# A gated feed-forward block whose gate and up products are formed by Strassen's seven block products, in a ring of four single PSUM banks

## The chip, the cores and the metric

The kernel runs on one core of one Trainium2 chip. Its metric is the device time of one execution in microseconds (us). The core has a matrix engine (TensorE; PE in the profile, its weight loads PEld), three engines for elementwise work (VectorE or DVE, ScalarE or ACT, GpSimd or POOL) and SyncE (SP), which here only issues transfers. Each engine takes its instructions in the order in which the kernel gives them, and semaphores between the engines hold an instruction back until its inputs, and the buffer that it writes, are ready. TensorE writes only to PSUM, which has eight banks of 512 fp32 columns; POOL works in SBUF only.

## The reference

Two residual blocks follow each other on an input of 2048 tokens by 640 features, in fp32. The first one is spectral: a layer norm, a two-dimensional real FFT, a product with a complex filter, the inverse FFT. The second is a bilinear gated feed-forward block without a nonlinearity:

```python
def _B_ref(x, w_gate, w_up, w_down):
    g = jnp.einsum("bsd,df->bsf", x, w_gate)
    u = jnp.einsum("bsd,df->bsf", x, w_up)
    h = g * u
    return jnp.einsum("bsf,fd->bsd", h, w_down)

x = A_x
h = x + _A_ref(_layernorm(x, axis=-1), A_w_r, A_w_i)
h2 = h + _B_ref(_layernorm(h, axis=-1), B_w_gate, B_w_up, B_w_down)
```

The inner width is 1728, that is 13 column blocks of 128 and a last one of 64.

## The kernel before

All tokens stay in SBUF as 16 tiles X[0..15] of 128 tokens. The spectral part works through three stages: a transform over tokens (lines 250 to 283), a loop over 16 groups of columns (lines 388 to 420: `d_mm`, `s2_mm`, `filt`, `is2_mm`, `is2_out`), and the inverse over features, tile by tile (lines 578 to 594: `id_mm`, `unfold`, `is1_mm`, `acc`). The last stage also takes the layer norm of the second block for the tiles 0 to 7 along (`scale_shift`, `normalise`), and turns the tiles by TensorE so that features lie on partitions (`turn_mm`, then `turn_hi` on ACT and `turn_lo` on DVE).

Precision is kept by splitting. Each fp32 operand of the feed-forward block is held as a high part of fewer bits (fp32r) and a low part, value minus high. A product is three matmuls that accumulate in one PSUM bank: high by high, high by low, low by high. ACT makes the high part by a copy, POOL (for weights) or DVE (for activations) the low part by a subtraction.

The feed-forward block runs in two halves of 1024 tokens (`blk`), each of two quarters of 512 tokens (`sb`), which are the moving operand of a matmul. `xt` holds the turned tokens: [128 features, sb, 5 pieces of 128 features, high or low, 512 tokens]. The 14 column blocks c are taken in pairs, p = 0 to 6, c = 2p and 2p+1. For each c and each quarter `gu` (line 530) forms gate and up in the two banks of a pair of banks, 2 matrices x 5 pieces x 3 matmuls of 128x512; the block 13 holds gate and up in 64 columns each, 15 matmuls. Then `gate` (line 602) lets ACT copy up out of PSUM, DVE multiply, ACT write the product's high part into `hts` and DVE its low part. `down` (line 617) multiplies one tile of 128 tokens by the pair's two rows of blocks of the down weights, 12 matmuls of 128x320 (10 for the last pair), and DVE adds the result to X (`acc`, line 480). In the step of pair p the eight downs of the pair before it are issued between the two quarters of its first block, so that an even block has downs beside it and an odd block has none.

The order of the work is written out by hand: the lists `aside`, `dside` and `tside` say what ACT, DVE and the turning do in each round of the last spectral stage; `fill` is a queue of small layer norm operations of the tiles 8 to 15, of which one is issued after each down (`pop`); `late` is a gate's last subtraction, issued after other work. At the end of the first half (`close`, `turn`; lines 691 to 713) normalising, turning and downs of the tiles 8 to 15 are interleaved.

Weights come through `load_w` (line 428): SP loads a block of 128x1280 into one of two `stage` buffers, ACT writes the high part, POOL the low part, into one of two `wgu` (or `wd`) buffers. Block c+2 is loaded after block c. PSUM has two pairs of banks for gate and up (tag `eo`) and two for the downs (tag `y`). Working tiles of 640 columns come from a ring of six (`wk`).

Of the kernel before, what the change touches and what calls it, by code (L numbers as in the profile page):

```python
# [46 lines left out]
def tile_spectral_glu(ctx: ExitStack, tc: tile.TileContext, x, wf, wgu, wlast, wdown, wdlast,  # L47
# [6 lines left out]
    phase = ExitStack()  # L54
    stream = phase.enter_context(tc.tile_pool(name="stream", bufs=3))
# [4 lines left out]
    held = [None, None]  # L60

    def banks(name):
        if held[0]:
            held[0].close()
        held[0] = ExitStack()
        held[1] = held[0].enter_context(tc.tile_pool(name=name, bufs=2, space=bass.MemoryType.PSUM))

    def bank(tag, bufs=2):
        return held[1].tile([P, 512], F32, tag=tag, name=tag, bufs=bufs)

    def pair(tag, bufs=2):
        return held[1].tile([P, 2, 512], F32, tag=tag, name=tag, bufs=bufs)
# [20 lines left out]
    cit = keep.tile([P, P], F32, name="cit")  # L93
    ident = keep.tile([P, P], F32, name="ident")
    imt = keep.tile([P, 4, 161], F32, name="imt")
    irt = keep.tile([P, 5, NQ], F32R, tag="ic", name="irt")
    fmt = stream.tile([P, 675], F32, name="fmt", bufs=1)
    frt = stream.tile([P, 2, 2, NQ], F32R, name="frt", bufs=1)
    s1 = keep.tile([P, 4, NG, P], F32, tag="big", name="s1")
    s1r = keep.tile([P, 2, NG, P], F32R, tag="rem", name="s1r", bufs=2)  # L100
    fold = keep.tile([P, NR * 1026 + 2 * D], F32, tag="qm", name="fold")
# [95 lines left out]
    def scale_c(t):  # L197
        CR[t] = small.tile([P, P], F32, tag="cr", name="cr")
# [21 lines left out]
    banks("pone")  # L220
# [66 lines left out]
    def load_wm(g):  # L287
        m = stream.tile([P, 2, P], F32, name="mt")
        w = stream.tile([P, 2, 2, NQ], F32, name="wt")
        nc.sync.dma_start(m, mm[g, :, 0])  # L290
        nc.sync.dma_start(w, wf[g])
        WM[g] = (m, w)

    def load_wi(g):
        WI[g] = stream.tile([P, 2, P], F32, name="wi")
        nc.sync.dma_start(WI[g], mm[g, :, 1])

    qm = keep.tile([P, 4, NT, P], F32, tag="qm", name="qm")
    qr = keep.tile([P, 2, NT, P], F32R, tag="rem", name="qr", bufs=2)
# [8 lines left out]
    def d_mm(g):  # L308
        ps = PD[g] = bank("re"), bank("im")
        cut = ((1, 0), (0, 0), (1, 160), (0, 160))  # L310
        main = [(b, o, FW[c], s1[:, c, g], fmt[:, FOFF[c]:FOFF[c] + FW[c]]) for c, (b, o) in enumerate(cut)]
# [63 lines left out]
    def is2_out(g):  # L375
        pm, pr = PI[g]
        f = small.tile([1, P], F32, tag="f", name="f")
# [17 lines left out]
    for g in range(NG - 1):  # L395
        s2_mm(g)
        if g + 2 < NG:
            d_mm(g + 2)
        if g == NG - 2:
# [14 lines left out]
        if g == 6:  # L414
            nc.gpsimd.dma_start(irt, irem)
# [5 lines left out]
    phase.close()  # L421
    make_identity(nc, ident)

    wpool = ctx.enter_context(tc.tile_pool(name="wpool", bufs=2))
    xt = keep.tile([P, 2, 5, 2, 512], F32R, tag="big", name="xt")
    W = {}

    def load_w(key, src, n, engine=nc.gpsimd):
        st = wpool.tile([P, 1280], F32, tag="stage", name="stage")
        nc.sync.dma_start(st[:, :n], src)  # L430
        if key[0] == "d":
            w = keep.tile([P, 2, 1280], F32R, tag="rem", name="wd", bufs=2)
        else:
            w = wpool.tile([P, 2, 1280], F32R, tag="wgu", name="wgu")
        W[key] = w
        cuts = [(a, min(n, a + 640)) for a in range(0, n, 640)]
        his = [lambda a=a, b=b: act(w[:, 0, a:b], st[:, a:b], AF.Copy) for a, b in cuts]  # L437
        los = [lambda a=a, b=b: engine.tensor_tensor(w[:, 1, a:b], st[:, a:b], f32(w[:, 0, a:b]), op=OP.subtract)  # L438
               for a, b in cuts]
        return his, los  # L440

    def load_gu(c, engine=nc.gpsimd):
        if c < NC - 1:
            return load_w(("g", c), wgu[c], 1280, engine)
        else:
            return load_w(("g", c), wlast, 640, engine)

    def load_d(p):
        return load_w(("d", p), wdown[p] if p < 6 else wdlast, 1280)
# [54 lines left out]
    def turn_mm(t, tag="y"):  # L504
        ps = PT[t] = pair(tag)
        pv = ps.rearrange("p a b -> p (a b)")
        for k in range(5):
            nc.tensor.transpose(pv[:, k * P:(k + 1) * P], Z[t][:, k * P:(k + 1) * P], ident)  # L508

    def turned(t, l):  # L510
        sb, i = divmod(t % 8, 4)
        return (xt[:, sb, :, l, i * P:(i + 1) * P],
                PT[t].rearrange("p a b -> p (a b)")[:, 0:640].rearrange("p (k s) -> p k s", k=5))

    def turn_hi(t):
        hi, pk = turned(t, 0)
        act(hi, pk, AF.Copy)

    def turn_lo(t):
        lo, pk = turned(t, 1)  # L520
        tt(lo, pk, f32(turned(t, 0)[0]), op=OP.subtract)  # L521

    def transp(t, tag="y"):
        turn_mm(t, tag)
# [5 lines left out]
    def gu(c, sb, which=(1, 0), ks=range(5)):  # L530
        if 1 in which:
            ps = pair("eo")
            PG[c, sb] = ps[:, 0], ps[:, 1]
        w = W["g", c]
        if c < NC - 1:
            wv = w.rearrange("p l (k m f) -> p l k m f", k=5, m=2)
            sel = [(PG[c, sb][m], lambda l, k, m=m: wv[:, l, k, m]) for m in which]
        else:
            wv = w[:, :, 0:640].rearrange("p l (k f) -> p l k f", k=5)
# [7 lines left out]
    banks("pthree")  # L547
# [308 lines left out]
```

## Time and profile before

| | us |
|---|---|
| median of 3 runs | 764.21 |
| lowest and highest | 764.11, 769.02 |
| profiled execution, its own time | 764.33 |
| its span in the profile | 762.6 |

Busy times in the span: PE 742.3, PEld 645.1, DVE 321.5, ACT 264.5, POOL 171.0 us. The profile's page gives busy time by engine, the span in 40 slices, the transfer queues, the chain of work that ended last, and the costliest groups of instructions. A row of a group gives the source line, the engine, the operation, output and input by the program's names with their shapes, the count, then the busy time, the mean duration of one in ns, and the idle time of the engine ahead of them with what ended it. All matmuls of the feed-forward block are issued by one helper and so have line 81; their tiles tell them apart (`eo<-xt,wgu` gate and up, `y<-wd,hts` down). Rows of the timeline give the start in us, the time until the last of the merged instructions ended, the engine, the group and the count. A matmul's recorded duration overlaps the one behind it, so a matmul's price is read from start to start over many.

The feed-forward block begins on TensorE at about 178 us.

### The profile page before, as it was taken

To read this page: it belongs to the slowest core of one execution; us is meant where nothing else is said; L and a number is where in the kernel's file an instruction comes from. 1 tells how busy PE (TensorE), PEld (TensorE's weight loads), DVE (VectorE), ACT (ScalarE), POOL (GpSimd) and SP (SyncE) were. 2 spreads that over 40 slices of the span, in tenths; PEclk is the share of its full clock that TensorE was granted. 3 is DMA by queue.
4 is the path that set the end of the run, shared out by engine and by line. 5 is a ranking of instruction groups with operands and counts; after the bars stand their busy time and mean duration, and the time that the engine had idled before them with its cause. 6 is when DMAs were issued, how large, how long until landed. Compare 5 with 4: busy or idle time off the path is not lost.

```text
span 762.6 us, 9943 instructions
## 1 busy us (share of the span) xinstructions
PE 742.3 (97%) x4028; PEld 645.1 (85%) x4028; DVE 321.5 (42%) x595; ACT 264.5 (35%) x517; POOL 171.0 (22%) x156
## 2 busy tenths in 40 slices
PE   6899997999999999999999999999999999999998
PEld 5789886988898888989898988888898989898887
DVE  7956665896232322425241335332232414132334
ACT  4759997364412222031212335222203121212201
POOL 3301113331613122131113031312212121313000
PEclk9999999999999999999999999999999999999999
DMA  9305762100311111111101002411101111210003
GB/s 339 139 8 188 247 206 94 59 2 1 114 59 59 46 36 69 35 35 35 69 36 52 35 0 104 176 68 35 69 35 36 35 69 35 70 35 17 1 1 139
DMA packets 18622, 55.05 MB, mean 72 GB/s; under 512 B 2064, under 2 KB 6672, under 8 KB 18576
## 3 DMA queue, kind: packets, MB, share of 16 engines
q1 hardware_dynamic: 18000, 52.69, 19.8%
q0 software_dynamic: 288, 1.48, 0.5%
q8 instruction: 32, 0.52, 0.3%
q10 hardware_dynamic: 288, 0.23, 0.1%
q14 instruction: 14, 0.11, 0.0%
HBM read 49.16 MB, written 5.24 MB: 71 GB/s over the span
## 4 chain that ended last, share of the span: by engine, by line
PE 83%; ACT 7%; DVE 7%; issue 1%; DMA 1%; DVEq 0%; ACTq 0%
PE eo L81 51%; PE y L81 26%; ACT us L332 1%; ACT us L333 1%; DVE fold L178 1%; PE re L81 1%; PE im L81 1%; ACT qm L383 1%; DVE fold L183 1%; PE re L249 1%; PE u L325 1%; DVE x L485 1%; PE eo L508 1%; ACT qr L380 1%; ACT t L318 1%
## 5 line engine op out<-in xcount | busy, mean ns | idle before, releaser
L81 PE MATMUL eo<-xt,wgu 128*128 128x512 f32 x1620 | 381.6, 395 | 0.0
L81 PEld LDWEIGHTS eo<-xt,wgu 128*128 128x128 f32 x1620 | 302.8, 187 | 73.1 <-DVE xt L521 0.5
L81 PE MATMUL y<-wd,hts 128*128 128x320 f32 x1312 | 196.4, 309 | 0.2 <-DVE x L483 0.2
L81 PEld LDWEIGHTS y<-wd,hts 128*128 128x128 f32 x1312 | 193.5, 188 | 1.7 <-DVE x L483 0.4
L609 DVE TENSOR_TENSOR hb<-eo,u 128x512 f32<-128x512 f32 x52 | 35.9, 691 | 275.4 <-ACT u L608 275.4
L483 DVE TENSOR_TENSOR x<-y,x 128x640 f32<-128x640 f32 x119 | 97.9, 823 | 77.3 <-PE y L81 77.0
L438 POOL TENSOR_TENSOR wgu<-stage,wgu 128x640 fp32r<-128x640 f32 x52 | 81.4, 1585 | 218.9 <-ACT wgu L437 218.8
L608 ACT ACTIVATE u<-eo 128x512 f32<-128x512 f32 x52 | 31.0, 596 | 230.1 <-PE eo L81 230.1
L438 POOL TENSOR_TENSOR wd<-stage,wd 128x640 fp32r<-128x640 f32 x28 | 43.3, 1569 | 192.1 <-ACT wd L437 192.1
L437 ACT ACTIVATE wd<-stage 128x640 fp32r<-128x640 f32 x28 | 19.2, 732 | 130.7 <-PE y L81 118.0
L611 DVE TENSOR_TENSOR hts<-hb,hts 128x512 fp32r<-128x512 f32 x52 | 37.5, 721 | 27.2 <-ACT hts L610 27.2
L610 ACT ACTIVATE hts<-hb 128x512 fp32r<-128x512 f32 x52 | 32.9, 632 | 39.6 <-DVE hb L609 39.6
L437 ACT ACTIVATE wgu<-stage 128x640 fp32r<-128x640 f32 x54 | 36.7, 724 | 4.4 <-DMA stage<-in_wgu_dram 4.4
L194 PE MATMUL u<-cr,fold 128*128 128x128 f32 x192 | 29.5, 291 | 4.6 <-POOL fold L168 1.2
L194 PEld LDWEIGHTS u<-cr,fold 128*128 128x128 f32 x192 | 24.5, 193 | 8.9 <-DVE fold L183 4.2
L472 POOL TENSOR_TENSOR yt<-q 128x318 f32<-128x318 f32 x16 | 16.3, 1020 | 32.4 <-DVE q L469 21.4
L81 PE MATMUL eo<-imt,qm 128*128 128x161 f32 x128 | 20.4, 301 | 0.7 <-ACT qm L383 0.7
L385 POOL CAST qr<-f 1x128 fp32r<-1x128 f32 x16 | 4.5, 280 | 73.6 <-DVE qr L382 73.5
L336 DVE TENSOR_TENSOR y<-u,wt 128x322 f32<-128x322 f32 x30 | 14.8, 493 | 14.3 <-ACT us L333 9.2
L81 PEld LDWEIGHTS eo<-imt,qm 128*128 128x128 f32 x128 | 18.5, 190 | 2.6 <-issue 0.9
L325 PE MATMUL u<-t,mt 128*128 128x322 f32 x60 | 19.9, 453 | 0.6
L81 PE MATMUL y<-yt,cit 128*128 128x320 f32 x64 | 19.6, 432 | 0.0
(140 smaller groups left out, 593.6 us busy)
## 6 DMA issues: line engine op xcount, KB each, us to landing
stage<-in_wgu_dram SPq DMA_DIRECT2D x26, 640.0 KB, 3.9
wt<-in_wf_dram SPq DMA_DIRECT2D x16, 644.0 KB, 4.0
stage<-in_wdown_dram SPq DMA_DIRECT2D x12, 640.0 KB, 3.9
x<-in_x_dram SPq DMA_DIRECT2D x16, 320.5 KB, 6.5
out_dram<-x SPq DMA_DIRECT2D x15, 320.0 KB, 2.2
mt<-in_mm_dram SPq DMA_DIRECT2D x16, 128.0 KB, 3.8
wi<-in_mm_dram SPq DMA_DIRECT2D x16, 128.0 KB, 4.0
stage<-in_wdlast_dram SPq DMA_DIRECT2D x2, 640.0 KB, 3.8
```

The costliest lines, as they stand in the source:

```text
L81: nc.tensor.matmul(o, l, r, start=start, stop=stop, skip_group_check=True)
L194: nc.tensor.matmul(pm[:, k * P:(k + 1) * P], l, c, start=n == 0, stop=n == len(ls) - 1)
L325: nc.tensor.matmul(ps[h][:, 0:NQ], WM[g][0][:, h], T[g][:, h], start=True, stop=True)
L336: tt(y[:, h], ps[h][:, 0:NQ], w[:, 0, h], op=OP.mult)
L437: his = [lambda a=a, b=b: act(w[:, 0, a:b], st[:, a:b], AF.Copy) for a, b in cuts]
L438: los = [lambda a=a, b=b: engine.tensor_tensor(w[:, 1, a:b], st[:, a:b], f32(w[:, 0, a:b]), op=OP.subtract) for a, b in cuts]
L472: nc.gpsimd.tensor_tensor(view(y, 639, [[-320, 2], [-1, 159]]), q[:, 0::2, 1:160], q[:, 1::2, 1:160], op=OP.subtract)
L483: tt(xv, ps[:, :, 0:320], xv, op=OP.add)
L608: act(u, pu, AF.Copy)
L609: tt(hb, pg, u, op=OP.mult)
L610: act(hh, hb, AF.Copy)
L611: return lambda: tt(hl, hb, f32(hh), op=OP.subtract)
```

## The change

Twelve of the fourteen column blocks (0 to 11) are formed in another way in each half. The first four pieces of the 640 features are taken as two pairs, the two quarters of tokens as two columns, gate and up as two rows: a product of two 2x2 matrices of blocks, which Strassen's scheme in the form with shared sums does in seven block products instead of eight. The fifth piece of features is added to four of the products as before. Blocks 12 and 13 are formed directly as before, and come first in each half (`order = [6, 0, 1, 2, 3, 4, 5]`).

The operands of the seven products are prepared. For the tokens, `turn_hi` copies the first four pieces of the tiles 0 to 3 of a half also as fp32 (`TJ["b"]`), `turn_lo` of the tiles 4 to 7 adds two differences (`TJ[j]`), and `t_rest`, `t12` and `t34` form the remaining differences and split them, on DVE and ACT. The fifth piece of the later tiles is turned apart (`fifth`). For the weights, `prep(c)` works on one staging buffer: ACT and POOL split four pieces (1024 columns), POOL forms the combinations in place in the staging buffer by four operations, then ACT and POOL split 896 and 256 columns of these. The first part of `prep(c+1)` is issued after the second product of block c, the second part after its sixth; the load of block c+2 follows block c.

The products go in the order 1, 6, 7, 5, 3, 2, 4, each into one bank of a ring of four; the sums that turn them into gate and up, and the product of the two, are done by DVE in place in PSUM, with four working tiles (`p1`, `u2`, `u3`, `c22`) per block. `hts` has three slots of one block in place of two of two. The downs of the pair before are issued inside an even block: two after product 5, two after product 3, four after product 4; the last pair's downs follow at the end, the tile 7 last. At the start of the second half the tiles 8 to 15 are normalised in one piece inside block 11, and turned between the downs of the last pair.

Buffers are assigned by hand to named places (`home`), most of which are used again by later stages; the tables of the spectral part lie in such places, and the inverse table `irt` is loaded into the place of `xt`, after the last forward transform of the columns.

```diff
+    def single():
+        return bank("e", 4)
...
-            nc.gpsimd.dma_start(irt, irem)
...
+        if g + 3 == NG:
+            xt = home("big", [P, 2, 5, 2, 512], "xt", F32R)
+            irt = xt[:, 1].rearrange("p k l n -> p (k l n)")[:, 0:5 * NQ].rearrange("p (c q) -> p c q", c=5)
+            nc.gpsimd.dma_start(irt, irem)
...
     def turn_hi(t):
         hi, pk = turned(t, 0)
         act(hi, pk, AF.Copy)
+        if t % 8 == 0:
+            TJ["b"] = home("dA", [P, 4, 4, P], "bt")
+        if t % 8 < 4:
+            act(TJ["b"][:, t % 4], pk[:, 0:4], AF.Copy)
 
     def turn_lo(t):
         lo, pk = turned(t, 1)
         tt(lo, pk, f32(turned(t, 0)[0]), op=OP.subtract)
+        if t % 8 >= 4:
+            j = t % 4
+            d = TJ[j] = wk([P, 4, P], "tj")
+            b = TJ["b"][:, j]
+            tt(d[:, 0:2], pk[:, 0:2], b[:, 0:2], op=OP.subtract)
+            tt(d[:, 2:4], pk[:, 2:4], d[:, 0:2], op=OP.subtract)
...
+    def t_rest(j):
+        b = TJ["b"][:, j].rearrange("p (a k) n -> p a (k n)", a=2)
+        tt(b, b, view(TJ[j], 256, [[0, 2], [1, 256]]), op=OP.subtract)
...
+        def first():
+            wa, ws = W[c] = slot_of(c, blk)
+            act(wa[:, 0], stage[:, 0:1024], AF.Copy)
+            ptt(wa[:, 1], stage[:, 0:1024], f32(wa[:, 0]), op=OP.subtract)
+            ptt(stage[:, 640:896], stage[:, 640:896], stage[:, 1024:1280], op=OP.add)
+            ptt(stage[:, 896:1280], stage[:, 256:640], stage[:, 896:1280], op=OP.subtract)
+            ptt(stage[:, 384:640], stage[:, 640:896], stage[:, 384:640], op=OP.subtract)
+            ptt(stage[:, 0:256], stage[:, 0:256], stage[:, 384:640], op=OP.subtract)
+
+        def second():
+            wa, ws = W[c]
+            for a, b, o in ((384, 1280, 0), (0, 256, 896)):
+                act(ws[:, 0, o:o + b - a], stage[:, a:b], AF.Copy)
+            for a, b, o in ((384, 1280, 0), (0, 256, 896)):
+                ptt(ws[:, 1, o:o + b - a], stage[:, a:b], f32(ws[:, 0, o:o + b - a]), op=OP.subtract)
...
+        o1 = product(wa, 384, b11)
+        p1, u2 = wk([P, 512], "p1"), wk([P, 512], "u2")
+        act(p1, o1, AF.Copy)
+        o6 = product(ws, 0, t2)
+        at(0)
+        if ahead:
+            ahead[0]()
+        tt(u2, o6, p1, op=OP.add)
+        at(1)
+        o7 = product(ws, 640, [(t3[:, k, 0], t3[:, k, 1]) for k in range(2)])
+        u3, c22 = wk([P, 512], "u3"), wk([P, 512], "c22")
+        tt(u3, u2, o7, op=OP.subtract)
+        o5 = product(ws, 256, t1, [(wa, 896, b5[1])])
+        tt(u2, o5, u2, op=OP.add)
+        tt(c22, o5, u3, op=OP.add)
+        some(2)
+        at(2)
+        o3 = product(ws, 896, b22, [(ws, 512, b5[1])])
+        tt(o3, o3, u2, op=OP.add)
+        tt(o3, o3, c22, op=OP.mult)
+        act(hh[1], o3, AF.Copy)
+        at(3)
+        some(1)
+        tt(hl[1], o3, f32(hh[1]), op=OP.subtract)
+        some(1)
+        o2 = product(wa, 0, b21, [(wa, 256, b5[0])])
+        if ahead:
+            ahead[1]()
+        tt(p1, o2, p1, op=OP.add)
+        o4 = product(wa, 640, t4, [(wa, 896, b5[0])])
+        some(1)
+        tt(o4, o4, u3, op=OP.add)
+        tt(o4, o4, p1, op=OP.mult)
+        act(hh[0], o4, AF.Copy)
+        at(4)
+        some(2)
+        tt(hl[0], o4, f32(hh[0]), op=OP.subtract)
+        some(8)
+        at(5)
+
+    order = [6, 0, 1, 2, 3, 4, 5]
...
+            t1s = [t12(j) for j in range(4)]
+            late = gate_parts(NC - 2, 0, s12)
+            for j in range(4):
+                t1s[j][0]()
+                t_rest(j)
+            late()
+            gu(NC - 1, 1)
+            for j in range(4):
+                t1s[j][1]()
+            wdn = load_d(p)
+            late = gate_parts(NC - 1, 1, s13)
+            hi, lo = t34(0)
+            hi()
+            late()
+            lo()
+            if blk == 0:
+                second()
+            gu(NC - 2, 1)
+            gate_parts(NC - 2, 1, s12)()
+            for f in t34(1):
+                f()
+            issue(wdn)
...
+                side[2] = [lambda: low(range(8))]
```

In this diff `at(n)` issues what a block takes along at that place (the down weights' split at 3, the eight normalisations at 2, the next load at 5), `some(n)` up to n downs with what `fill` holds, `product` three matmuls for each pair of a weight piece and a token operand.

More of the change, by code (lines that the diff above doesn't have):

```diff
@@ L218, in s1_lo @@
            op=OP.subtract)
-    banks("pone")
+    banks("a", "pone")
     dve = [[] for _ in range(NT)]
@@ L643, in down @@
         acc(t, ps)
[L644 removed]
+        if last:
             nc.sync.dma_start(rows(out, t), X[t])
[L647 to L663 removed]
@@ L673, in tile_spectral_glu @@
         for ci in range(2):
             c = 2 * p + ci
-            first, turn, close = ci == 0 and n > 0, ci == 0 and n == 7, blk == 0 and c == NC - 1
-            if n or ci:
-                gu(c, 0)
-            late = gate(c, 0, slot, ci)
-            if first:
-                downs(prev, (4,) if turn else (0,))
-            late()
-            if n == 6 and ci == 0:
-                pop(len(fill))
-                for k in range(8, 12):
-                    lower(k)
-            if n == 0 and ci == 0:
-                issue(load_gu, 1)
-                issue(load_d, 0)
@@ L729, in tables @@
+            strassen(c, blk, slots[ci], ahead, downs if ci == 0 else [], side)
+            count += 1
+        prev = (blk, p, slots)
+    for j in (4, 5, 6, 0, 1, 2, 3, 7):
+        down(*prev, j, True)
+    open_pools["a"].close()
+    open_pools["y"].close()
 def tables():
```

368 lines of the change are left out of this document (213 added, 155 removed).

## The prediction

> **What bounds the kernel now.** First the page's busy times and slices, then the groups, then the engines by stretch, then the timeline of one step.
>
> ```profile
> span 762.6 us, 9943 instructions
> PE 742.3 (97%) x4028; PEld 645.1 (85%) x4028; DVE 321.5 (42%) x595; ACT 264.5 (35%) x517; POOL 171.0 (22%) x156
> PE 83%; ACT 7%; DVE 7%; issue 1%; DMA 1%; DVEq 0%; ACTq 0%
> ```
>
> TensorE is busy 97% of the span and holds 83% of the chain that ended last. Where, the stretches say:
>
> ```profile
> core 0: us, PE busy (x) PEld busy (x) DVE busy (x) ACT busy (x) POOL busy (x), PEclk, DMA share, GB/s
> 150.00:178.00 28.00, 27.39 (x162) 23.02 (x162) 26.70 (x71) 16.81 (x35) 8.99 (x9) 1.00 0.08 25
> 178.00:200.00 22.00, 22.00 (x104) 17.63 (x104) 8.84 (x14) 8.07 (x12) 7.13 (x5) 1.00 0.09 31
> 452.00:482.00 30.00, 29.81 (x179) 26.56 (x178) 17.17 (x23) 15.06 (x22) 6.19 (x4) 1.00 0.27 99
> 500.00:550.00 50.00, 50.00 (x251) 42.94 (x251) 13.42 (x18) 11.28 (x18) 12.39 (x8) 1.00 0.11 40
> ```
>
> The granted clock (column PEclk) is 1.00 throughout. From 178 us on TensorE never rests, with DVE, ACT and POOL near a quarter full. Before that, in the last spectral stage, DVE is as full as TensorE (26.70 of 28). The turn between the halves (452 to 482) costs 0.2. What one matmul costs there:
>
> ```profile
> L81 PE MATMUL eo<-xt,wgu 128*128 128x512 f32 x1620 | 381.6, 395 | 0.0
> L81 PEld LDWEIGHTS eo<-xt,wgu 128*128 128x128 f32 x1620 | 302.8, 187 | 73.1 <-DVE xt L521 0.5
> L81 PE MATMUL y<-wd,hts 128*128 128x320 f32 x1312 | 196.4, 309 | 0.2 <-DVE x L483 0.2
> 386.59 14.24 PE L81 MATMUL y<-wd,hts 128*128 128x320 f32 x96
> 400.67 28.16 PE L81 MATMUL eo<-xt,wgu 128*128 128x512 f32 x120
> 428.67 11.60 PE L81 MATMUL y<-wd,hts 128*128 128x320 f32 x78
> ```
>
> The mean of 395 ns overlaps its neighbour; from start to start 120 gate/up matmuls take 428.67 - 400.67 = 28.00 us, 0.2333 each, and 96 down matmuls 400.67 - 386.59 = 14.08, 0.1467 each. A step of two column blocks is 42.08 us.
>
> **The TensorE term.** A full column block needs 2 token halves x 2 matrices x 5 x 3 = 60 matmuls now. By Strassen it is seven products of 2 x 3 plus four pieces of 3 for the fifth part of D: 54. Twelve blocks in each half change, 12 and 13 do not: 24 x 6 = 144 fewer, 1620 to 1476. The 1312 down matmuls and the 80 transpositions stay. 144 x 0.2333 = **33.6 us less**. The Trainium skill ("TensorE: Matmul & The Clock Gate", "Back-to-back issue gap") gives about 131 ns as the sustained spacing of 512-column matmuls; by it the saving would be 18.9 us and the time 760.5. The trace does not agree: its 233 ns decides.
>
> **What takes its place, in the odd blocks.** A block with downs beside it lasts 7 products and 8 downs, 26.7 us. An odd one (c = 2p+1) has no downs: 54 x 0.2333 = 12.6 us, in which the next block's weights must be made. Its prices:
>
> ```profile
> L609 DVE TENSOR_TENSOR hb<-eo,u 128x512 f32<-128x512 f32 x52 | 35.9, 691 | 275.4 <-ACT u L608 275.4
> L608 ACT ACTIVATE u<-eo 128x512 f32<-128x512 f32 x52 | 31.0, 596 | 230.1 <-PE eo L81 230.1
> L610 ACT ACTIVATE hts<-hb 128x512 fp32r<-128x512 f32 x52 | 32.9, 632 | 39.6 <-DVE hb L609 39.6
> L437 ACT ACTIVATE wgu<-stage 128x640 fp32r<-128x640 f32 x54 | 36.7, 724 | 4.4 <-DMA stage<-in_wgu_dram 4.4
> L438 POOL TENSOR_TENSOR wd<-stage,wd 128x640 fp32r<-128x640 f32 x28 | 43.3, 1569 | 192.1 <-ACT wd L437 192.1
> L168 POOL TENSOR_TENSOR fold<-x 128x320 f32<-128x320 f32 x16 | 14.1, 891 | 19.8 <-DVE fold L183 8.4 <-DMA x<-in_x_dram 5.4 <-DVE ve L126 1.7
> stage<-in_wgu_dram SPq DMA_DIRECT2D x26, 640.0 KB, 3.9
> stage<-in_wlast_dram SPq DMA_DIRECT2D x2, 320.0 KB, 2.9
> L483 DVE TENSOR_TENSOR x<-y,x 128x640 f32<-128x640 f32 x119 | 97.9, 823 | 77.3 <-PE y L81 77.0
> 386.85 0.60 ACT L608 ACTIVATE u<-eo 128x512 f32<-128x512 f32 x1 [3.75 <-PE eo L81]
> ```
>
> POOL's two rows give 2.12 ns an element and 0.21 us a call: 1024 columns 2.38 us, 896 2.11, 384 1.03, 256 0.75. ACT's give 1 ns for each further element: 1024 1.11, 896 0.98. TensorE's result reaches the next engine 0.26 after the next matmul starts (386.85 to 386.59). From the block's start: products 1, 6, 7, 5, 3, 2, 4 end at 1.40, 2.80, 4.20, 6.30, 8.40, 10.50, 12.60. ACT copies product 1 (to 2.26), splits 1024 weights (to 3.37); POOL subtracts and forms four combinations, 2.38 + 3 x 0.75 + 1.03 = 5.66, to 9.1. DVE adds and multiplies on product 3 (8.66 to 10.08), ACT writes its high part (to 10.75) and, behind that in its queue, splits 896 combined weights (to 11.64); POOL subtracts them by 13.8, the last 256 by 14.6. The next block's second product wants those low weights at its third matmul, 12.60 + 1.40 + 0.47 = 14.47: **0.65 spare**. Product 4's bank is wanted again three products into the next block, 16.8; add, multiply, high part and low part release it at 15.7: 1.1 spare. The staging buffer refills from 14.6 and lands at 18.5, 5.9 into the long block; behind ACT's wait for it stands nothing before product 3's high part at 13.6. There POOL's 5.66 end at 11.7, the down weights' split (two of 1.57, behind ACT's part at 14.9) at 18.1, the combined weights at 21.1, and the next load lands at 25.0, before the odd block begins at 26.7. On SP the down weights (two loads of 2.9) stand behind the staging load: there by 8, wanted at 14. The adds are 11 DVE operations of 0.69 a block where there were four, 7.6 us; with eight accumulations of 0.82 a pair takes 21.8 of 39.3 us on DVE. So I take **0** for the steady state, and what gives way if the cover goes is TensorE, at once. DVE writing PSUM in place has no row. Excluding a time below a read's, it costs from 0.69 (the nearest row, taken) to twice that; then the chain is 1.4 longer, 0.7 late in each of 12 odd blocks, 9 us.
>
> **The spectral stage.** DVE sets its pace, so a third weight split and the differences for token block 4 count in full: 1.37 + 2 x 0.42.
>
> ```profile
> L438 DVE TENSOR_TENSOR wgu<-stage,wgu 128x640 fp32r<-128x640 f32 x2 | 2.7, 1372 | 0.0
> L382 DVE TENSOR_TENSOR qr<-ir,qr 64x256 fp32r<-64x256 f32 x14 | 5.9, 418 | 10.3 <-ACT f L381 10.3
> 117.16 0.31 PE L81 MATMUL im<-frt,s1r 128*128 128x322 f32 x1
> 131.72 0.58 PE L81 MATMUL eo<-irt,qr 128*128 128x322 f32 x2
> irt<-in_irem_dram POOLq DMA_DIRECT2D x1, 805.0 KB, 7.2
> ```
>
> Four ACT copies beside them lie within ACT's idle (16.81 busy of 28). **+2.0**, between 0 and 4.6 (with these copies at 0.6). The inverse table's load moves behind the last column transform (117.5), on POOL; it lands at 124.7, needed at 131.7: nothing. POOL's queue behind it holds one-row casts that nothing waits for before the last stage. SP's loads keep their ring of three, so the retagged buffers cost nothing.
>
> **The start of the first half.** Blocks 13 and 12 now run here with no downs, on four banks. I followed the queues, from 0 at the transposition of token block 4 (177.82 now).
>
> ```profile
> 177.82 0.77 PE y L508 x5
> 178.59 3.50 PE eo L81 x15
> 182.09 1.08 PE y L81 x4
> 201.29 3.10 POOL L438 TENSOR_TENSOR wd<-stage,wd 128x640 fp32r<-128x640 f32 x2 [1.81 <-ACT wd L437]
> 374.87 0.69 DVE L611 TENSOR_TENSOR hts<-hb,hts 128x512 fp32r<-128x512 f32 x1 [0.70 <-ACT hts L610]
> 204.49 3.43 POOL L438 TENSOR_TENSOR wgu<-stage,wgu 128x640 fp32r<-128x640 f32 x2
> 205.63 0.69 DVE L609 TENSOR_TENSOR hb<-eo,u 128x512 f32<-128x512 f32 x1 [0.69 <-ACT u L608]
> 207.02 1.45 DVE L611 TENSOR_TENSOR hts<-hb,hts 128x512 fp32r<-128x512 f32 x1 [0.70 <-ACT hts L610]
> 456.69 1.73 ACT L500 ACTIVATE zc<-x,b,r 128x640 f32<-128x640 f32 x2
> ```
>
> While POOL works, a DVE operation with both inputs in SBUF takes 1.45 instead of 0.69; one that reads PSUM does not slow down. (The Trainium skill, "SBUF — State Buffer", "Who interferes with whom", says that the former contends with POOL's reads and the latter does not; the trace agrees.) Strassen's adds read PSUM; the operand differences do not.
> - Block 12. TensorE: transposition 0.5, block 13 3.5, three inverse transforms 3.2, three transpositions of four 1.3, fifteen matmuls 3.5: at 12.0 it wants the bank that block 13's gate still reads. DVE: token block 5 (split 0.69, two differences 0.84) to 7.85, accumulation, gate product, accumulation to 10.2, a wait for ACT to 10.65, token blocks 6 and 7 (3.1), the gate's low part: 14.45. Wait **2.5**.
> - Its second token half. TensorE is at 14.5 + 3.5 + 0.4 (the fifth pieces) + 3.5 (block 13) + 3.5 = 25.4. ACT copies the fifth pieces, splits weights (20.2) and copies block 12 (20.8), DVE multiplies (21.5); then four differences at 1.45 beside POOL's weights (27.3) stand ahead of the low part that frees the bank: 28.0. Wait **2.6**.
> - Product 6 of block 0. TensorE wants its low weights at 28.0 + 3.5 + 1.4 + 0.47 = 33.4. DVE: four low parts, a product to 31.5; ACT: high part 32.1, operand split 33.2, combined weights 34.2; POOL 36.4. Wait **3.0**.
> - Product 7's bank, released 37.95 where TensorE is at 37.3: **0.65**. The down weights of blocks 12 and 13, split on POOL from 39.0 to 42.2, wanted at 41.45: **0.8**.
>
> Together **+9.5**; before, that stretch had no wait at all. It lies between 0 (the order of ready work may absorb them) and 19 (every late queue twice as late).
>
> **The turn.** Eight normalisations now stand in ACT's queue in one piece, 8 x 0.865 = 6.9 us (the row of two: 1.73), behind product 5 (from 6.56 after block 11's start to 13.5) and ahead of the high part of product 3, whose low part then ends on DVE at 14.9 and frees the bank. TensorE has done product 4 at 12.6 and the first transposition at 13.0, and wants that bank for the second: 1.9. The third down then wants a pair of banks whose accumulation stands on DVE behind the new tiles' splits (21.0 for 20.2): 0.8. Block 12's second half wants a bank that its first half's gate, behind four differences at 0.69, leaves 0.9 later. Sum 3.6 against 0.2 now, **+3.4**, between 0 and 7. The last down has 12 matmuls instead of 10, half of it behind the last bank: +0.15.
>
> **The sum** is made against the profiled execution's own 764.33 (span 762.6 and 1.73 around it; 0.12 above the median): 764.33 - 33.6 + 2.0 + 9.5 + 3.4 + 0.15 = **745.8 us**.
>
> **The rivals.** A, *all starts hidden*: 764.3 - 33.6 = 730.7. For it: 35 to 42% busy engines have room; against: the queues above are in order, and the banks fell to singles.
> B, *odd blocks a little late*: the chain misses by 0.7 to 1.2 us, 12 times, up to 14: 754 to 760. For it: 0.65 spare is thin; against: POOL's rows repeat to 0.02 us.
> C, *slower*: POOL's preparation becomes the bound. In odd blocks POOL's 5.66 and 2.11 us both stretch by a factor f; the later one ends at 3.45 + 7.77f. For 14.47 + 1.55 (12 x 1.55 = 18.5, the whole gain) f must be 1.62. At f = 2, 4.5 late, 12 times: 800. For it: DVE's 1.45; against: POOL's pair went only from 3.10 to 3.43 there, f = 1.1.
> D, *the matmuls saved are worth less*: if the weight loads set the pace, a matmul saved is worth its load, 0.187: 26.9 instead of 33.6, 752.5. For it: the loads are busy 85% of the span; against: spacing goes with the moving columns (0.2333 at 512, 0.1467 at 320) at equal loads.
>
> **Chances.** Forecast 0.55, A 0.17, B 0.16, C 0.07, D 0.05. Faster by over 1% (about what a measurement of this kernel tells from no change) means under 756.6: the forecast but for an upper tail 0.51, A 0.17, a part of B 0.06, D less its tail 0.04: 0.78. Slower: C's upper part, 0.05. The rest, 0.17. The range leaves out A's end and C, and takes in D and B up to 759: 734 to 759; the likeliest case alone is 738 to 752.
>
> **What would show it.** Right: 1476 matmuls of 128x512 at 0.233; 39.3 us per pair of blocks; TensorE waits of 2 to 3 us by DVE and POOL at the start of the first half, near 2 at the turn. Wrong: a TensorE wait repeating every 39 us (B; above 1.5 us each, C), none anywhere (A), a saving per matmul under 0.2 us (D).

## The result, and the profile after

The changed kernel takes 735.0 us (median of 4 runs, 734.25 to 737.35) where the kernel before takes 766.4 on the same chip (764.11 to 769.02). The ratio is 0.959, 95% interval 0.955 to 0.964. Forecast were 745.8 us, 734 to 759. The profiled execution took 734.25 us, 732.5 of them span.

Some executions, of the kernel before too, are 1 to 5 us longer, with one more fall of the clock in the spectral part; two of the four behind the 766.4 are of this kind, and the account below sets 764.33 against 734.25, both without it.

The page of the changed kernel:

```profile
span 732.5 us, 10144 instructions
PE 704.9 (96%) x3884; PEld 620.4 (85%) x3884; DVE 454.4 (62%) x803; ACT 277.9 (38%) x540; POOL 299.5 (41%) x275
...
PEclk9999999999989999999999999999999999999999
```

TensorE is still busy 96% of the span. DVE rose from 321.5 to 454.4 us and POOL from 171.0 to 299.5, and neither became the bound. New is the digit 8 among the clocks, in the twelfth of the 40 slices (201 to 220 us). The groups of TensorE with 512 columns, with the count ahead of the bar:

```profile
L82 PE MATMUL e<-xt,wst 128*128 128x512 f32 x864 | 206.8, 390 | 0.0
...
L82 PE MATMUL e<-t,wst 128*128 128x512 f32 x288 | 74.9, 395 | 4.3 <-ACT wst L693 2.7 <-POOL wst L695 1.6
L82 PE MATMUL e<-xt,wdir 128*128 128x512 f32 x180 | 41.9, 391 | 1.1 <-DVE q L475 1.1
L82 PE MATMUL e<-ht,wst 128*128 128x512 f32 x144 | 37.8, 399 | 0.0
```

864 + 288 + 180 + 144 = 1476 matmuls of 512 columns, as counted ahead. What one costs is read from start to start. This is the timeline of one pair of blocks in the steady state; the second column reaches to the end of the last matmul and is not the price:

```profile
315.62 1.55 PE L82 MATMUL e<-xt,wst 128*128 128x512 f32 x6
317.01 1.52 PE L82 MATMUL e<-t,wst 128*128 128x512 f32 x6
318.37 1.52 PE L82 MATMUL e<-ht,wst 128*128 128x512 f32 x6
...
325.47 0.60 ACT L790 ACTIVATE ht<-e 128x512 fp32r<-128x512 f32 x1 [6.72 <-DVE e L789]
...
326.99 2.82 POOL L695 TENSOR_TENSOR wst<-raw,wst 128x896 fp32r<-128x896 f32 x2 [2.19 <-ACT wst L693]
...
329.25 1.52 PE L82 MATMUL e<-t,wst 128*128 128x512 f32 x6
...
334.01 3.68 PE L82 MATMUL y<-wd,ht 128*128 128x320 f32 x24
337.52 2.23 PE L82 MATMUL e<-xt,wst 128*128 128x512 f32 x9
...
354.24 1.55 PE L82 MATMUL e<-xt,wst 128*128 128x512 f32 x6
```

Six matmuls take 318.37 - 317.01 = 1.36 us: **0.2267 each, where the kernel before needed 0.2333**. A down matmul stayed at (337.52 - 334.01) / 24 = 0.146. The pair takes 354.24 - 315.62 = 38.62; 108 x 0.2267 + 96 x 0.1467 are 38.56. So nothing waits there. The forecast of 39.3 was right about the waits and wrong about the price.

The longest waits of TensorE from 178 to 240 us (in total, times, longest), and the busy times of a stretch behind them:

```profile
PE e L82 <- ACT wst L693: 2.7, 1, 2.7
PE e L82 <- POOL wst L695: 1.6, 1, 1.6
PE e L82 <- DVE q L475: 1.1, 1, 1.1
```

```profile
core 0: us, PE busy (x) PEld busy (x) DVE busy (x) ACT busy (x) POOL busy (x), PEclk, DMA share, GB/s
212.65:225.00 12.35, 12.35 (x51) 10.52 (x52) 6.93 (x11) 3.48 (x5) 9.80 (x8) 0.77 0.31 108
```

TensorE stands still for 2.70 and 1.63 us, and then it is slow: from 212.65 to 225 it is busy throughout and its granted clock is 0.77 on average (more exactly, one half up to 218.21 and full behind it). The start of the first half shows both:

```profile
188.47 7.18 PE L82 MATMUL e<-xt,wdir 128*128 128x512 f32 x30
...
193.25 0.68 DVE L639 TENSOR_TENSOR ht<-e,ht 64x512 fp32r<-64x512 f32 x1
...
195.74 10.48 PE L82 MATMUL e<-xt,wdir 128*128 128x512 f32 x45
...
198.59 5.62 DVE L556 TENSOR_TENSOR bt<-bt,tj 128x512 f32<-128x512 f32 x4
...
206.06 1.52 PE L82 MATMUL e<-xt,wst 128*128 128x512 f32 x6
210.28 0.73 PE L82 MATMUL e<-t,wst 128*128 128x512 f32 x2 [2.70 <-ACT wst L693]
212.65 2.07 PE L82 MATMUL e<-t,wst 128*128 128x512 f32 x4 [1.63 <-POOL wst L695]
214.52 2.76 PE L82 MATMUL e<-ht,wst 128*128 128x512 f32 x6
219.68 3.09 PE L82 MATMUL y<-wd,ht 128*128 128x320 f32 x20
```

The 19 matmuls from 212.65 to 219.68 take 7.03 us; at 0.2267 they are 4.31. The fall of the clock costs 2.7 us there. In the turn between the halves two waits are left:

```profile
445.02 0.66 PE L518 MATMUL e<-ident,zt 128*128 128x128 f32 x4 [0.67 <-DVE ht L793]
451.00 2.03 PE L82 MATMUL y<-wd,ht 128*128 128x320 f32 x12 [0.49 <-DVE x L489]
```

**The account.** Against a run in which every stretch takes its matmuls' price, the changed kernel loses 0.8 us ahead of the first transposition of token block 4 (178.64, was 177.82), 1.6 to 206.06, 8.2 from there to 238.27 (32.21 us where the matmuls' price is 23.97), 1.9 in the turn, 1.1 in the steady stretches and 0.9 at the end: 14.5. The kernel before lost 1.1 in the same way, 0.4 of it in the turn and 0.6 at the end. So 764.33 - 33.6 (144 matmuls fewer) - 9.8 (the other 1476 cheaper by 0.00667 each) + 13.4 = 734.3, and 734.25 were measured. The forecast had no 9.8, and 15.05 in place of 13.4.

### The profile page after: what moved, and what is told of

It is laid out like the page before. It is cut to its first block, busy times and chain, and to the rows that moved or that the text cites. A ratio compares the mean times of both kernels' runs of the same rounds, so it can differ in the third digit from the quotient of the medians.

```text
span 732.5 us, 10144 instructions
## 1 busy us (share of the span) xinstructions
PE 704.9 (96%) x3884; PEld 620.4 (85%) x3884; DVE 454.4 (62%) x803; ACT 277.9 (38%) x540; POOL 299.5 (41%) x275
## 4 chain that ended last, share of the span: by engine, by line
PE 77%; DVE 11%; ACT 10%; issue 1%; DMA 1%; POOL 0%; DVEq 0%; ACTq 0%
PE e L82 44%; PE y L82 26%; PE eo L82 2%; ACT us L343 2%; ACT us L344 2%; DVE fold L190 1%; ACT qm L394 1%; PE re L261 1%; DVE x L489 1%; DVE fold L195 1%; DVE bt L556 1%; PE im L82 1%; PE re L82 1%; ACT t L331 1%; ACT t L330 1%
## 5 line engine op out<-in xcount | busy, mean ns | idle before, releaser
L82 PE MATMUL e<-xt,wst 128*128 128x512 f32 x864 | 206.8, 390 | 0.0
L82 PE MATMUL y<-wd,ht 128*128 128x320 f32 x1312 | 201.4, 310 | 1.2 <-DVE x L489 1.1
L82 PEld LDWEIGHTS y<-wd,ht 128*128 128x128 f32 x1312 | 195.3, 188 | 5.7 <-DVE x L489 2.7
L82 PEld LDWEIGHTS e<-xt,wst 128*128 128x128 f32 x864 | 160.7, 188 | 31.7
L684 POOL TENSOR_TENSOR wst<-raw,wst 128x1024 fp32r<-128x1024 f32 x24 | 57.8, 2409 | 169.6 <-ACT wst L683 169.6
L695 POOL TENSOR_TENSOR wst<-raw,wst 128x896 fp32r<-128x896 f32 (+1 forms) x48 | 67.9, 1438 | 27.8 <-ACT wst L693 27.8
L82 PE MATMUL e<-t,wst 128*128 128x512 f32 x288 | 74.9, 395 | 4.3 <-ACT wst L693 2.7
L82 PEld LDWEIGHTS e<-t,wst 128*128 128x128 f32 x288 | 55.0, 191 | 16.7 <-ACT wst L693 3.1
L445 POOL TENSOR_TENSOR wd<-draw,wd 128x640 fp32r<-128x640 f32 x28 | 44.4, 1608 | 47.7 <-ACT wd L444 47.7
L82 PE MATMUL e<-xt,wdir 128*128 128x512 f32 x180 | 41.9, 391 | 1.1 <-DVE q L475 1.1
```

What stands on the lines that cost most here:

```text
L82: nc.tensor.matmul(o, l, r, start=start, stop=stop, skip_group_check=True)
L445: los.append(lambda r=r, a=a, b=b: engine.tensor_tensor(w[:, 1, a:b], r, f32(w[:, 0, a:b]), op=OP.subtract))
L684: ptt(wa[:, 1], stage[:, 0:1024], f32(wa[:, 0]), op=OP.subtract)
L695: ptt(ws[:, 1, o:o + b - a], stage[:, a:b], f32(ws[:, 0, o:o + b - a]), op=OP.subtract)
```

## The experiments

Two things were to be explained: why a matmul became cheaper, and what the start of the first half really loses.

**Why 0.2267.** The same matmul, with the same operand shapes, became 7 ns shorter. The change gives the weight buffers other sizes and thereby other places in SBUF. In the kernel before the moving operand starts 32 bytes past a multiple of 64 and the weights on one; in the changed kernel both start 32 past. (Distance means below: the start of the weights less that of the moving operand, as it lies past a multiple of 256 bytes. It is 224 in the kernel before and 0 in the changed one.) My first theory was that equal places past a multiple of 64 bytes make the difference. The rival was that something in the order of the products does. The first run moves the buffers of the kernel before and changes nothing else:

```diff
+    padding = ctx.enter_context(tc.tile_pool(name="padding", bufs=1))
+    nc.gpsimd.memset(padding.tile([P, 8], F32, name="pad"), 0.0)
...
```

> The kernel before, with one unused strip of 32 bytes ahead of the gate and up weights, so that their high and low parts start 32 bytes past a 64-byte line, as the moving tokens already do. Nothing else moves on TensorE. Theory, place in SBUF: the spacing of the 128x512 matmuls falls from 0.2333 to the 0.2267 of the changed kernel, 1620 x 0.0067 = 10.8 us less, about 753.5. Rival, the single PSUM banks or the new layout of the weights made the matmuls faster: spacing stays 0.2333 and the time about 764.

Measured: 755.58 us against 764.64, ratio 0.987 (0.983 to 0.990).

```profile
398.14 27.39 PE L81 MATMUL eo<-xt,wgu 128*128 128x512 f32 x120
425.36 4.85 PE L81 MATMUL y<-wd,hts 128*128 128x320 f32 x32
```

120 matmuls now take 425.36 - 398.14 = 27.22 us, 0.2268 each, where they took 28.00. 32 bytes of padding are worth 9 us to the kernel before. The reverse, the changed kernel with its weights 32 bytes further on in their buffers:

```diff
-        w = home("wB" if (c + blk) % 2 == 0 else "wA", [P, 4352], "wst", F32R)
-        return cut(w, 0, 2, 1024), cut(w, 2048, 2, 1152)
+        w = home("wB" if (c + blk) % 2 == 0 else "wA", [P, 4368], "wst", F32R)
+        return cut(w, 8, 2, 1024), cut(w, 2056, 2, 1152)
```

(`wdir` likewise: [P, 3856], its parts at 8 and 1288. The larger buffers also move what lies behind them, so that the distances in this run are 32, 96, 160 and 224.)

> The changed kernel with only the gate and up weights moved by 32 bytes within their buffers, onto a 64-byte line, while the tokens stay 32 bytes past one: the offsets of the kernel before. Place in SBUF: spacing 0.2333 in all 1476 matmuls, 9.8 us more, about 744. Rival, single banks: spacing 0.2267, 734.

Measured: 743.06 us (742.53 to 743.67), 8.1 more than the changed kernel. Six matmuls take 320.86 - 319.46 = 1.40 again:

```profile
319.46 1.56 PE L82 MATMUL e<-t,wst 128*128 128x512 f32 x6
320.86 1.56 PE L82 MATMUL e<-ht,wst 128*128 128x512 f32 x6
```

The third run puts both operands on multiples of 64 bytes and leaves the distance at 0 (32 bytes of padding ahead of both, and a table ahead of both widened by 64):

```diff
+    nc.gpsimd.memset(keep.tile([P, 8], F32, name="pad"), 0.0)
...
-    tab = home("stage", [P, 1448], "tab")
+    tab = home("stage", [P, 1464], "tab")
```

> The changed kernel with a strip of 32 bytes ahead of all reused buffers, so that tokens, weights, products and down weights all start on a 64-byte line. If only an equal offset of the two operands matters: spacing 0.2267 and 0.1467 as now, 734. If the moving operand also pays for its own offset: 512 columns below 0.220 and 320 columns below 0.140, 12 to 25 us less, 710 to 722. If neither matters: 734.

Measured: 734.76 us, the spacing still 1.36 for six. So a start on a multiple of 64 bytes is worth nothing; the place of the one relative to the other counts. The modulus of 64 was only a guess so far, and a later run was made to test it, with another shift in every odd block:

```diff
-        return cut(w, 0, 2, 1024), cut(w, 2048, 2, 1152)
+        o = (0, 1, 0, 2, 0, 4, 0, 8, 0, 16, 0, 32)[c]
+        return cut(w, o, 2, 1024), cut(w, 2048 + o, 2, 1152)
```

> The changed kernel with the weights of the odd column blocks alone shifted inside their buffer, by another distance in each: block 1 by 4 bytes, 3 by 8, 5 by 16, 7 by 32, 9 by 64, 11 by 128 (the staged matrix's even blocks stay). Where weights and moving columns start at the same distance past a multiple of 64 bytes, six matmuls take 1.36 us, where they differed by 32 they took 1.39 to 1.40. Theory, only equality past a multiple of 64 bytes counts: blocks 1, 3, 5 and 7 at 1.40 a product, 9 and 11 and all even blocks at 1.36; eight slow blocks of 54 matmuls give 432 x 0.006 = 2.6 us, 737.6. Rival, the price comes in steps of 32 bytes: block 7 alone slow (and 0.7 us in all, 735.7). Rival, it depends on the distance between the operands as a whole: 9 and 11 slow too.

Measured: 739.67 us (one run), 4.7 more than the changed kernel, and not as expected. In the first half, blocks 9 and 11, shifted by 64 and 128 bytes, were slow as well, and so were even blocks with no shift: the buffers had grown by 128 bytes, and this had moved one of the two by 128 against the tokens. An even block shows it by itself. Its products 6 and 7 use the same weights buffer, with moving operands from two buffers; the distance is 128 for product 6 and 0 for product 7:

```profile
291.46 1.56 PE L82 MATMUL e<-t,wst 128*128 128x512 f32 x6
292.86 1.54 PE L82 MATMUL e<-ht,wst 128*128 128x512 f32 x6
294.23 1.55 PE L82 MATMUL e<-t,wst 128*128 128x512 f32 x6
```

Product 6 takes 292.86 - 291.46 = 1.40 and product 7 294.23 - 292.86 = 1.37. So the rule must have 256 in it, not 64, and that was put to a test in which the two rules forecast different things: the padding of the first run at 96 and at 288 bytes (the second line with 72 in place of 24):

```diff
-    nc.gpsimd.memset(padding.tile([P, 8], F32, name="pad"), 0.0)
+    nc.gpsimd.memset(padding.tile([P, 24], F32, name="pad"), 0.0)
```

> The kernel before with its weight buffers 96 bytes further on (the first run moved them by 32). From the weights' start to that of the moving columns it is then 64 bytes past a multiple of 256, and 0 past a multiple of 64. Theory after the run by blocks, the spacing is 0.2267 us only where the two starts are equal past a multiple of 256 bytes: no gain, 0.2333 and 764 to 765 us. The older theory, equal past a multiple of 64 bytes is enough: 0.2267 and 755.6.

> The same with 288 bytes: the two starts are then equal past a multiple of 256 bytes (and of 512). Both theories: 0.2267 us and 755.6, as the first run (32 bytes, equal past a multiple of 256 as well). A third, that only the very place of the first run is good: 764 to 765.

Measured: 765.15 us with 96 bytes (ratio 0.999, 0.997 to 1.001) and 754.79 with 288 (0.987, 0.983 to 0.991). The first two rows are of 96 bytes, the others of 288:

```profile
401.87 28.17 PE L81 MATMUL eo<-xt,wgu 128*128 128x512 f32 x120
429.87 10.42 PE L81 MATMUL y<-wd,hts 128*128 128x320 f32 x70
```

```profile
396.71 27.39 PE L81 MATMUL eo<-xt,wgu 128*128 128x512 f32 x120
423.94 14.24 PE L81 MATMUL y<-wd,hts 128*128 128x320 f32 x96
```

28.00 and 27.23 us for 120. The older theory fell. Where weights and moving operand start equally far past a multiple of 256 bytes, 512 columns settle at 0.2267 us in every run. At most other distances tried they take 0.231 to 0.2333 (whole kernels at 64 and 224; blocks at 4, 8, 16, 32, 96, 128, 136, 144 and 160), and some 0.229 at 192. But the run by blocks also has an exception, which the two theories leave out. In its second half, block 1 has its weights at a distance of 132. The first row holds thirty of its matmuls and six of the next block, at 0:

```profile
517.93 8.32 PE L82 MATMUL e<-xt,wst 128*128 128x512 f32 x36
526.09 1.52 PE L82 MATMUL e<-t,wst 128*128 128x512 f32 x6
```

526.09 - 517.93 = 8.16 us for 36 is the low price, 0.2267, while the six matmuls ahead of them, also at 132, took 0.233 each. So an equal place is enough for the low price and is not shown to be needed. Why the chip does so no run shows.

**What the start of the first half loses.** TensorE waits 4.3 us for the combined weights of block 0, and the clock falls. The theory: DVE's and POOL's queues are late, and the clock falls because TensorE stands still. The first attempt issues those weights ahead of block 13's second gate:

```diff
             late()
+            if blk == 0:
+                second()
             gu(NC - 1, 1)
...
             lo()
-            if blk == 0:
-                second()
```

> The changed kernel with the second part of block 0's weight preparation issued ahead of block 13's second token half in the first half, not behind the operand split. Theory: product 6 of block 0 waits for these weights (2.70 for ACT, 1.63 for POOL) and the granted clock falls behind that wait; both go, 4.3 + 2.7 = 7 us less, about 727, clock 1.00 throughout. Rival: the clock falls for what runs there, not for the wait: 4.3 less, 730, with a stretch at about 0.8 left. Second rival: the split moved up holds back block 13's gate on ACT and the wait only moves there: 733.

Measured: 733.86 us, against 735.0 within the spread. The weights are early now, and TensorE waits almost as long for something else:

```profile
205.56 4.94 DVE L560 TENSOR_TENSOR t<-tj,t 128x512 fp32r<-128x512 f32 x4
...
212.49 2.93 PE L82 MATMUL e<-t,wst 128*128 128x512 f32 x6 [4.09 <-DVE ht L639]
```

The four low parts of L560 now run beside POOL's subtractions and take 4.94 us where they took 2.48, and the low part of L639 stands behind them and holds the bank. The clock fell here too (0.87 from 212.65 to 225), for half as long. The wait had moved, so the thing to remove was the late work on DVE. The four differences of L556 (5.62 us at 198.59) need nothing that isn't there at 193.9; they only stood behind the split of the fifth pieces, which waits for TensorE:

```diff
     late()
+    for j in range(4):
+        t_rest(j)
     gu(NC - 2, 0)
     fifth((5, 6, 7))
...
                 t1s[j][0]()
-                t_rest(j)
+                if blk == 1:
+                    t_rest(j)
```

> The four DVE differences of L556 of the first half (1.4 us each beside POOL, 198.59 to 204.2) move ahead of the fifth pieces, into DVE's idle stretch from 193.9 to 196.6. Theory, DVE's and POOL's queues make the wait: the four take 0.7 each, everything behind them on DVE ends some 2.9 us earlier, the combined weights' high part ends near 208.1 instead of 210.3 and the low part near 210.4 instead of 212.6; TensorE wants them at 207.4 and 208.5, so 0.7 + 1.9 = 2.6 of wait is left where there were 4.3, and the time is 735.0 less 1.7 to 3, about 732.5. Rival, another wait takes its place as in the run before: 734 to 735.

Measured: median 731.13 us; 729.49 and 729.57 in two executions, 732.69 and 733.08 in the others, the profiled one among them, whose clock was 0.64 between 125 and 135 us. Its times below lie some 4 us later for that reason.

```profile
198.25 2.50 DVE L556 TENSOR_TENSOR bt<-bt,tj 128x512 f32<-128x512 f32 x4
...
214.06 1.20 PE L82 MATMUL e<-t,wst 128*128 128x512 f32 x4 [1.63 <-POOL wst L697]
215.09 1.53 PE L82 MATMUL e<-ht,wst 128*128 128x512 f32 x6
```

The four take 2.50 us in place of 5.62. The wait for ACT's high part is gone, that for POOL's low part is the old 1.63, and the four matmuls behind it take 215.09 - 214.06 = 1.03 us where they took 1.87: the clock holds (1.00 from 206 on). From the first product of block 0 to that of block 1 this trace takes 237.09 - 210.33 = 26.76 us in place of 32.21: 5.5 less, 2.7 for the wait and about as much for the clock. The two short executions are 4.7 below the 734.25; where the other 0.7 went isn't shown. Both edits together:

> The same, and the combined weights of block 0 earlier as in the run before. Theory that two late things stood one behind the other, and that the clock fell because TensorE paused: low weights are there by 207.7 and block 13's second gate frees its bank near 206.5, so under 0.5 us of wait is left of 4.33; the granted clock stays at 0.99 or over from 205 to 225 us, where it was 0.90 and 0.77; 4 + 2.7 gained, 728.3. Rival, the clock falls there for another reason (the hour of the run, the load of the other engines): 0.77 again, 731. Rival, the wait moves a third time: 733 to 735.

Measured: median 729.79, three of the four within 729.34 to 730.14. No wait for the weights is left, but four small ones of 0.57, 0.44, 0.29 and 0.38 (the bank of block 13's second gate, that of block 12's, and the down weights) add up to 1.68, as much as the run before had. Its stretch in the place of the slow one:

```profile
212.65:225.00 12.35, 11.68 (x65) 10.21 (x64) 9.45 (x17) 4.59 (x8) 10.98 (x9) 1.00 0.01 2
```

The clock is 1.00. So the fall belongs to the pauses, and the thirteen traces together say more about it. In each of them the clock changes on a raster of 3.413 us, whose start differs from execution to execution: it is one half for one, two or three such steps, and full otherwise. The rows show single steps: the length, the time for which TensorE was busy, and the granted clock. The first two are of the changed kernel, the third of the run with the differences first, the last of the kernel before with 288 bytes of padding:

```profile
207.97:211.38 3.41, 0.73 (x2) 1.00 0.00 0
211.38:214.79 3.41, 2.15 (x5) 0.50 0.13 20
124.48:127.90 3.42, 1.52 (x15) 1.00 0.52 196
124.85:128.26 3.41, 1.54 (x12) 1.00 0.00 0
```

In the changed kernel TensorE stands still for 3.41 - 0.73 = 2.68 us of the step, and the clock is one half in the next. It also falls behind the third row, with 1.89 us, but not behind the fourth, with 1.87. Taken over all steps at full clock in the thirteen traces, up to the last matmul, a fall follows each of the twelve in which TensorE stands still for 1.89 us or more, and none of the others. So it is the idle time in sum within one step that goes with a fall, and not the length of one pause. This fits the spectral part too: all versions have a pause of 1.89 us there, which lies within one step in six traces, where the clock falls, and is cut by the end of a step in the other seven, where it doesn't. No run was made to test this, and other loads may have another limit.

**How thin the steady state is.** The forecast found 0.65 us spare on the combined weights in odd blocks. The trace has 0.63: the third matmul of product 6 starts at 329.25 + 2 x 0.2267 = 329.70, and POOL's 896 columns, which take 2.08 from 326.99 (2.82 less 0.74 for the last 256), end at 329.07. One more subtraction on POOL should show it:

```diff
+            if c > 0 and c % 2 == 0:
+                ptt(ws[:, 1, 0:640], stage[:, 384:1024], f32(ws[:, 0, 0:640]), op=OP.subtract)
             for a, b, o in ((384, 1280, 0), (0, 256, 896)):
                 ptt(ws[:, 1, o:o + b - a], ...)
```

> A subtraction of 640 columns (1.57 us) is repeated on POOL ahead of the low part of the combined weights, in the blocks without downs only: 10 in the run (the successors of c = 1, 3, 5, 7, 9 in each half). Theory, 0.63 us is spare there: TensorE waits 0.9 to 1.0 for POOL 10 times, 735.0 + 9.4 = 744.4, and a pair of blocks takes 39.5 us instead of 38.6. Rival, POOL has room that the trace does not show: 735. Rival, each wait also lowers the clock as the long one at 210 us did, by a few us each: above 755.

Measured: 746.31 us (745.79 to 746.55), 11.3 more. The wait list and one odd block:

```profile
PE e L82 <- POOL wst L697: 10.9, 11, 1.6
```

```profile
330.99 0.61 PE L82 MATMUL e<-t,wst 128*128 128x512 f32 x2
...
332.53 1.20 PE L82 MATMUL e<-t,wst 128*128 128x512 f32 x4 [0.93 <-POOL wst L697]
333.56 1.53 PE L82 MATMUL e<-ht,wst 128*128 128x512 f32 x6
```

10.9 less the 1.6 of the start are ten waits of 0.93, where 0.94 were worked out. Each costs more than its length: the product takes 333.56 - 330.99 = 2.57 instead of 1.36, 1.21 more. After a pause four matmuls take 1.03 in place of 0.91. Ten times 1.21 is 12.1, somewhat above the 11.3 measured. The clock did not fall behind these ten.

**The other waits.** The two edits that removed the wait for the weights, and two for waits elsewhere: block 13's first matmuls behind the inverse transform of their tile (the wait of 1.12 for L475), and the normalisations of the turn in two groups of four:

```diff
-            gu(NC - 1, 0)
         is1_mm(t)
+        if t == NT - 3:
+            gu(NC - 1, 0)
...
-                side[2] = [lambda: low(range(8))]
+                side[2], side[3] = [lambda: low(range(4))], [lambda: low(range(4, 8))]
```

> The last but one, with two more edits: block 13's first 15 matmuls stand behind token block 13's inverse transform instead of ahead of it (a TensorE wait of 1.12 for DVE at the reopened banks), and of the eight normalisations in block 11 four stand behind product 5 and four behind the high part of product 3 (waits of 0.67 and 0.49 at the turn). Theory, each wait has its own cause and none takes its place: 728.3 less 1.1 less 0.7 to 1.2, about 726.3. Rival, DVE paces the last spectral tiles anyway and ACT the turn: the two give nothing, 728.3.

Measured: 727.94 us (median of 6, 727.3 to 731.73), ratio to the kernel before 0.950 (0.947 to 0.953). That is 1.9 under the run with the first two edits, as expected. That run had come out 1.5 above its own expectation of 728.3, and so this one is 1.6 above the 726.3. The waits of 1.12 for L475 and of 0.67 for L793 are gone from the list. It is the fastest version of the study.

## Why the prediction was right, and where it was not

The forecast was 745.8 us, the time 735.0: inside the range, near its lower end, outside the likeliest case's own 738 to 752.

- **The matmuls saved: 33.6 us.** The count was right (1476). The step that failed is the price: "0.2333 each" was carried from the kernel before to the changed one, as if it belonged to the shape. It belongs to the shape and to the place of the operands. All 1476 became 0.0067 us cheaper, 9.8 us, by an accident of the buffers' sizes. Compared at equal places (the kernel before with 32 or 288 bytes of padding, 755.2 on average), the change gains 20.2 us: 144 x 0.2267 = 32.6 less 12.4 of costs. Rival D, a saved matmul worth its weight load of 0.187, is not what is seen: the spacing is 0.2267 with loads of 188 to 194 ns.
- **The steady state: 0.** Right, and with the right margins: 0.65 forecast and 0.63 found; 0.8 us were lost over some 415 us, without a wait on the list. Product 3's high part began 325.47 - 315.62 = 9.85 after the block's start, forecast were 10.08. DVE's writing in place into PSUM cost 0.70, the nearest row taken. Rivals B and C needed POOL or DVE longer than the rows said. The run with more work on POOL shows how near B was: 1.6 us more on POOL cost 11.3. The forecast counted 12 odd blocks a run; ten hand over to a block with staged weights.
- **The spectral stage: +2.0.** 0.8 measured up to the first transposition.
- **The start of the first half: +9.5.** 9.8 measured (1.6 and 8.2), for other reasons. Of the five waits only one came, that of product 6. The 2.5 and 2.6 for banks did not come, nor the 0.65 and 0.8 behind product 6, where TensorE was late and slow. For the first two I had dealt the four banks out in turn. In the trace block 12's 30 matmuls run through from 188.47 while the bank of block 13's gate is released only at 193.25 + 0.68; the groups took the banks of turned tiles, which were free earlier. The wait for the combined weights was 4.3 in place of 3.0, with the differences at 5.62 / 4 = 1.4 each beside POOL as forecast (1.45). The clock's 2.7 us were not in the sum at all: the granted clock of the kernel before was 1.00 in every stretch I had read, and it had no pause there. The wait for L475 (1.12) was not foreseen either. That this term came out near its size is luck.
- **The turn: +3.4.** 1.5 measured (1.9 less the 0.4 of the kernel before). Of the three waits two came, 0.67 for 1.9 and 0.49 for 0.8.
- **The end: +0.15.** 0.3 measured (0.9 less the 0.6 of the kernel before).

So the costs were about right in sum (13.4 for 15.05), in part by luck, and the forecast was off by the price per matmul.

## What to carry to other kernels

Before a duration is carried from one kernel to another, ask what besides its shape it may depend on; here it was the distance between two operands in SBUF, and a padding of 32 bytes was worth 1.3%, without any change of the work. When an edit removes a wait and the time stays, read what TensorE waits for now and look for the work that both waits stood behind: here the cure was not to start the awaited work earlier, but to move four subtractions into a gap ahead. Price a pause of TensorE above its length: by 0.3 us for a short one (1.21 for 0.93 here), and by the lost clock where pauses close to each other add up (2.7 us here for 2.68 of idle time within 3.41).

## What the runs showed of the hardware that was not expected

- The spacing of matmuls of 128x512 (fp32r) settles at 0.2267 us where weights and moving operand start equally far past a multiple of 256 bytes, and is 0.229 to 0.2333 at nearly all other distances tried; over 1476 of them that is up to 10 us. At 132 bytes both prices were seen. Matmuls of 320 columns stayed near 0.147 at distances of 0, 64, 128 and 192 bytes.
- The granted clock fell to one half for 6.83 us (a loss of 2.7 us) behind two pauses of 2.70 and 1.63 us with 0.73 us of work between them, and for 3.41 us behind one of 4.09 and, in some executions, behind one of 1.89 in the spectral part. In the thirteen traces it fell behind every step of 3.41 us with 1.89 us or more of idle time in sum, and behind no other. The Trainium skill ("TensorE: Matmul & The Clock Gate", "HAM oscillation — how this bites in real kernels") warns of gaps over about 3.4 us. Here shorter ones were enough.
- A DVE subtraction with both inputs in SBUF beside POOL's took 1.4 us in place of 0.63 (5.62 and 2.50 for four), and POOL's own of 256 columns 1.07 in place of 0.74: both sides pay.
